# Attention with a decay gate and a Gelu feed-forward on one core: one fused, interleaved pipeline in place of two stages with a DRAM hand-over

## The chip, the cores and the metric

The kernel runs on one core of a Trainium2 chip. The core has TensorE (PE; its weight loads are shown apart, as PEld), VectorE (DVE), ScalarE (ACT), GpSimd (POOL) and SyncE (SP), and 16 DMA engines that the queues of SP and POOL share. The metric is the device time in microseconds; that of the kernel before is 622.77 us, the median of 3 runs (622.64 to 623.76).

## The reference

Attention runs over 8 batches of 8 heads, 576 tokens of 64 numbers each; its output, as 4608 rows of 512, goes through two matrix products with an exact Gelu between them. Inputs and output are float32.

```python
scores = scale * np.matmul(q, k.transpose(0, 1, 3, 2))          # scale = 1/8
cum = np.cumsum(np.log(np.clip(f, 0.0001, 1.0)), axis=-1)
decay = cum[:, :, :, None] - cum[:, :, None, :]
scores = np.where(causal, -1000000000.0, scores + decay)
attn = softmax(scores)                                           # over keys
x = np.matmul(attn, v).transpose(0, 2, 1, 3).reshape(4608, 512)
out = gelu(x @ w_in) @ w_out                                     # 512 -> 2048 -> 512
```

The row term of the decay, `cum` of the query, cancels in the softmax, so a kernel needs only the key's term, exp(-cum).

## The kernel before

It has a short start and two stages. The order of the instructions on each engine is chosen by the framework's scheduler, not by the source.

**Start.** `f` is loaded, ACT takes the logarithm (L68), DVE makes the running sum in ten shifted additions (L72), and five transposes put its negative into `neg_cumT`, keys on partitions (L83, L86).

**Attention**, one head at a time, 64 heads. POOL's queue loads q, k and v with a cast to bf16, one DMA each, in rows of 64 numbers (L122). PE transposes q and k in blocks of 128 tokens (L141), ten transposes a head, and DVE copies them out of PSUM (L146). For each of the five key blocks, four of 128 keys and one of 64, PE computes the scores of the queries from that block on (L158): the contraction is over 64 rows, so the matmuls stand in the profile as 64*128. ACT takes the exponential with `neg_cumT` as a per-partition bias (L166), POOL zeroes the upper triangle of the diagonal block (L173). For each of five query blocks PE sums exp times v, with a 65th column of ones for the row sums, in 15 matmuls of 65 columns a head (L190); DVE divides (L198, L199), and SP stores 64 columns of x in DRAM (L202, L209).

**Feed-forward.** After the last head POOL's queue loads both weight matrices (L223, L224) and SP reads x back through transposing DMAs (L232). Nine chunks of 512 tokens then run one after the other: GEMM1, 16 groups of 4 matmuls of 512 columns (L244), each followed by a Gelu on ACT (L251); GEMM2, 4 groups of 16 such matmuls (L257), each copied out by ACT (L264), and one store of 1 MB a chunk (L265).

Of the kernel before, what the change touches and what calls it, by code (L numbers as in the profile page):

```python
# [10 lines left out]
Exp = mybir.ActivationFunctionType.Exp
Ln = mybir.ActivationFunctionType.Ln
Gelu = mybir.ActivationFunctionType.Gelu
is_ge = mybir.AluOpType.is_ge
# [3 lines left out]
def kernel(  # L19
# [11 lines left out]
    P = 128  # L31

    B, H, S, D = q.shape
# [1 line left out]
    assert D == 64 and S == 576 and BH == 64
# [4 lines left out]
    KB = 128  # L40
    blocks = []
    ss = 0
    while ss < S:
        ns = min(KB, S - ss)
        blocks.append((ss, ns))
        ss += ns
    NB = len(blocks)
# [6 lines left out]
    neg_cumT = consts.tile([P, NB, BH], FP32)

    with tc.tile_pool(name="pre", bufs=1) as pre, tc.tile_pool(
        name="pre_psum", bufs=2, space=bass.MemoryType.PSUM
    ) as pre_psum:
        ident_fp = pre.tile([P, P], FP32)
        make_identity(nc, ident_fp)  # L60
        f_sb = pre.tile([BH, S], FP32)
        nc.sync.dma_start(f_sb, f.rearrange("b h s -> (b h) s"))
        PAD = 512
        c0 = pre.tile([BH, PAD + S], FP32)
        c1 = pre.tile([BH, PAD + S], FP32)
        nc.vector.memset(c0[:, :PAD], 0.0)
        nc.vector.memset(c1[:, :PAD], 0.0)
        nc.scalar.activation(c0[:, PAD:], f_sb, Ln)  # L68
        shift = 1
        src, dst = c0, c1  # L70
        while shift < S:
            nc.vector.tensor_add(  # L72
                dst[:, PAD:], src[:, PAD:], src[:, PAD - shift : PAD - shift + S]
            )
            shift *= 2
            src, dst = dst, src
        cum = src[:, PAD:]
        negcum = pre.tile([BH, S], FP32)
        nc.scalar.mul(negcum, cum, -1.0)
        for n in range(NB):  # L80
            s0, ns = blocks[n]
            ps = pre_psum.tile([P, BH], FP32)
# [216 lines left out]
```

## Time and profile before

| | |
|---|---|
| median of 3 runs | 622.77 us |
| profiled execution, first to last instruction (its span) | 621.1 us |
| what lies around the span, median less span | 1.7 us |
| PE busy | 567.9 us, 91% |
| ACT busy | 272.3 us, 44% |
| POOL busy | 249.7 us, 40% |
| DVE busy | 189.5 us, 31% |
| DMA packets | 191776, of which 184497 under 512 bytes |

The trace holds one execution, and its span is the only time known of that execution itself. Rows of a group by line give line, engine, operation, names and shapes, count, then after the bar the busy time in us, the mean of one in ns, the idle time of the engine just before them and what ended most of it. For a matmul "64*128" is rows times columns of the array in use, and "128x512" the moving operand. The end of a matmul is modelled, so a busy PE is not a PE at its best; the distance from one start to the next says more. In rows of a timeline the first number is the start from the beginning of the span, the second the length, both in us.

### The profile page before, as it was taken

Reading aid. Unit: us, or ns where it says so; the run is one execution under the profiler, and the core shown is the slowest. Engines: PE = TensorE matmul, PEld = TensorE weight load, DVE = VectorE, ACT = ScalarE, POOL = GpSimd, SP = SyncE. Lnnn points to the kernel's source line nnn. Section 1 sums busy time; section 2 is a strip of 40 time slices with the busy share of each in tenths; the row PEclk is TensorE's granted clock in tenths of the full one; section 3 lists DMA queues with packets and bytes.
Section 4 is the critical chain, followed back from the end, with each engine's and each line's share of the span. In section 5 each row is a group of like instructions: output and inputs, shape, how many; then the busy total and the mean of one; then the engine's idle time right before and its main releaser. Section 6 shows DMA issues by size and latency. Waiting matters only on the chain.

```text
span 621.1 us, 9241 instructions
## 1 busy us (share of the span) xinstructions
PE 567.9 (91%) x3118; PEld 289.6 (47%) x3141; DVE 189.5 (31%) x849; ACT 272.3 (44%) x505; POOL 249.7 (40%) x525
## 2 busy tenths in 40 slices
PE   0799999999999999999995069999999999999996
PEld 0355555555555555555552024444444444444442
DVE  6244555556555565555655000000000000000000
ACT  2255455454454554545552043526253443526251
POOL 0989877777777778777742000000000000000000
PEclk9999999999999999999999999999999999999999
DMA  0999999899998889988723985501001010101001
GB/s 10 75 73 76 78 67 69 64 68 67 67 72 64 66 65 69 71 65 66 55 30 61 200 154 97 141 12 68 37 32 69 1 68 1 68 1 68 33 35 69
DMA packets 191776, 39.54 MB, mean 64 GB/s; under 512 B 184497, under 2 KB 186545, under 8 KB 191729
## 3 DMA queue, kind: packets, MB, share of 16 engines
q0 software_dynamic: 128400, 19.91, 43.6%
q1 hardware_dynamic: 63328, 19.04, 13.5%
q8 instruction: 25, 0.41, 0.3%
q14 instruction: 23, 0.18, 0.1%
HBM read 39.94 MB, written 14.16 MB: 87 GB/s over the span
## 4 chain that ended last, share of the span: by engine, by line
PE 89%; DMA 3%; DVE 2%; SPq 2%; ACT 2%; POOL 1%; issue 1%; ACTq 0%; POOLq 0%
PE ps L257 20%; PE ps L244 20%; PE sc L158 18%; PE ps L141 17%; PE o L190 14%; DMA xT_sb<-x_dram 2%; SPq L232 2%; DVE c L72 1%; ACT gT L251 1%; POOL q_bf L122 0%; DMA f_sb<-in_f_dram 0%; POOL k_bf L122 0%; ACT exp_sb L166 0%; POOL v_aug L122 0%; DMA x_dram<-out_head 0%
## 5 line engine op out<-in xcount | busy, mean ns | idle before, releaser
L166 ACT ACTIVATE exp_sb<-sc,neg_cumT 128x576 bf16<-128x576 f32 (+4 forms) x320 | 160.1, 526 | 156.2 <-POOL exp_sb L173 67.2
L244 PE MATMUL ps<-xT_sb,w_in_sb 128*128 128x512 bf16 x565 | 130.5, 383 | 25.8 <-issue 16.2
L158 PE MATMUL sc<-qT,kT 64*128 64x512 bf16 (+5 forms) x384 | 133.5, 410 | 1.2 <-DVE kT L146 0.5
L257 PE MATMUL ps<-w_out_sb,gT 128*128 128x512 bf16 x564 | 125.2, 379 | 0.6
L190 PE MATMUL o<-v_aug,exp_sb 128*128 128x65 bf16 (+2 forms) x960 | 120.9, 244 | 2.3 <-POOL exp_sb L173 1.0
L251 ACT ACTIVATE gT<-ps 128x512 bf16<-128x512 f32 x144 | 85.9, 597 | 42.2 <-PE ps L244 42.2
L244 PEld LDWEIGHTS <-w_in_sb 128*128 128x128 bf16 x576 | 56.1, 97 | 98.6 <-issue 37.5
L190 PEld LDWEIGHTS <-exp_sb 128*128 128x128 bf16 (+2 forms) x960 | 74.9, 131 | 53.6 <-DVE recip L198 26.2
L173 POOL TENSOR_SCALAR_AFFINE_SELECT exp_sb<-exp_sb 128x128 bf16<-128x128 bf16 (+1 forms) x320 | 86.8, 291 | 13.4 <-ACT exp_sb L166 10.0
L199 DVE TENSOR_SCALAR out_head<-o,recip 128x64 bf16<-128x64 f32 (+1 forms) x320 | 88.3, 276 | 5.5 <-DVE recip L198 0.3
L198 DVE RECIPROCAL recip<-o 128x1 f32<-128x1 f32 (+1 forms) x320 | 52.2, 163 | 121.3 <-PE o L190 116.2
L257 PEld LDWEIGHTS <-gT 128*128 128x128 bf16 x576 | 56.3, 98 | 68.0
L122 POOL DMA_DIRECT2D q_bf<-in_q_dram x63 | 54.7, 868 | 61.8 <-PE ps L141 44.4
L141 PE MATMUL ps<-ident_bf,q_bf 128*64 128x128 bf16 (+1 forms) x320 | 65.0, 302 | 3.8 <-issue 3.8
L264 ACT COPY out_sb<-ps 128x512 f32<-128x512 f32 x36 | 21.1, 586 | 102.7 <-PE ps L257 102.7
L141 PE MATMUL ps<-ident_bf,k_bf 128*64 128x128 bf16 (+1 forms) x320 | 58.4, 303 | 0.0
L158 PEld LDWEIGHTS <-kT 64*128 64x128 bf16 (+1 forms) x384 | 38.5, 115 | 39.3 <-issue 17.5
L122 POOL DMA_DIRECT2D v_aug<-in_v_dram x63 | 54.6, 866 | 4.7 <-PE o L190 4.4
L122 POOL DMA_DIRECT2D k_bf<-in_k_dram x63 | 54.5, 866 | 0.4 <-PE sc L158 0.2
L141 PEld LDWEIGHTS <-q_bf 128*64 128x64 bf16 (+1 forms) x320 | 34.2, 142 | 40.2 <-issue 27.5
L141 PEld LDWEIGHTS <-k_bf 128*64 128x64 bf16 (+1 forms) x320 | 33.3, 150 | 11.5 <-issue 3.2
L146 DVE COPY qT<-ps 64x576 bf16<-64x576 bf16 x64 | 28.8, 449 | 10.4 <-PE ps L141 8.7
(29 smaller groups left out, 55.3 us busy)
## 6 DMA issues: line engine op xcount, KB each, us to landing
out_dram<-out_sb SPq DMA_DIRECT2D x9, 1024.0 KB, 4.3
q_bf<-in_q_dram POOLq DMA_DIRECT2D x63, 80.0 KB, 2.9
k_bf<-in_k_dram POOLq DMA_DIRECT2D x63, 80.0 KB, 3.0
v_aug<-in_v_dram POOLq DMA_DIRECT2D x63, 80.0 KB, 2.9
x_dram<-out_head SPq DMA_DIRECT2D x64, 64.0 KB, 2.3
w_in_sb<-in_moe_w_in_dram POOLq DMA_DIRECT2D x1, 2048.0 KB, 13.6
w_out_sb<-in_moe_w_out_dram POOLq DMA_DIRECT2D x1, 2048.0 KB, 25.8
x_dram<-out_head SPq DMA_DIRECT2D x64, 8.0 KB, 1.7
```

What stands on the lines that cost most here:

```text
L122: nc.gpsimd.dma_start(dst, src_ap)
L141: nc.tensor.transpose(ps[:, n * KB : n * KB + ns], bfsrc[:ns, n, :], ident_bf[:ns, :ns],)
L146: nc.vector.tensor_copy(dst[:, :S], ps[:, :S])
L158: nc.tensor.matmul(sc[:ns, q_off : q_off + cw], kT[:D, s0n : s0n + ns], qT[:D, s0n + q_off : s0n + q_off + cw], start=True, stop=True,)
L166: nc.scalar.activation(exp_sb[:ns, :Qc], sc[:ns, :Qc], Exp, bias=neg_cumT[:ns, n : n + 1, bh : bh + 1], scale=scale,)
L173: nc.gpsimd.affine_select(out=exp_sb[:ns, :ns], in_=exp_sb[:ns, :ns], compare_op=is_ge, fill=0.0, base=0, pattern=[[1, ns]], channel_multi ...
L190: nc.tensor.matmul(o[:ms, : D + 1], exp_tiles[n][:ns, col : col + ms], v_aug[:ns, n, :], start=(n == 0), stop=(n == m),)
L198: nc.vector.reciprocal(recip[:ms, :], o[:ms, D : D + 1])
L199: nc.vector.tensor_scalar_mul(out_head[:ms, m, :], o[:ms, :D], recip[:ms, :1])
L244: nc.tensor.matmul(ps, w_in_sb[:, kt, ffb * P : (ffb + 1) * P], xT_sb[:, kt, t0 : t0 + TC], start=(kt == 0), stop=(kt == n_dm - 1),)
L251: nc.scalar.activation(gT[ffb], ps, Gelu)
L257: nc.tensor.matmul(ps2, gT[kt][:, tsub * P : (tsub + 1) * P], w_out_sb[:, kt, :], start=(kt == 0), stop=(kt == n_ff - 1),)
```

## The change

Everything between the constants and the last store is written anew; the lines that go are those printed above. The order on each engine is now that of the source (`manual_schedule`).

- **Loads.** q and k come for a whole batch in one DMA each, 96 partitions by rows of six tokens (384 numbers); v comes as float32 through SP's queue, with its 64 last tokens in a 128-token block from 448 on. Weights are loaded early, in four DMAs each.
- **Decay.** exp(cum at 288 - cum) is made once (a scan on DVE, Exp on ACT, five transposes into `wT`), and POOL multiplies v and the column of ones by it (`weigh_v`), so the exponential of the scores has no bias. All five key blocks have 128 keys; the doubled keys of the last have weight zero.
- **Two heads at a time**, 32 pairs. One transpose takes two tokens of a head, 128 columns on 96 rows (`transposes`), and four strided DVE copies put them in order. k of both heads lies on 128 partitions; q of each head lies on its half, the other half zero (`qA`, `qB`), so that every score matmul contracts over 128 rows. Scores go into four tiles of two PSUM banks, each with one ACTIVATE of up to 1024 numbers (`scores`, `STILES`).
- **x stays on the chip.** `normalize` writes x of a pair, `to_xT` transposes it on PE, and DVE copies it into `xT_sb`. The round trip through DRAM goes.
- **Interleaving.** Batch b's attention is issued with the matmuls of GEMM2 of chunk b-1 between its parts (`take(fill, n)`), then GEMM1 of chunk b with the q and k transposes and the weighing of batch b+1 in it. Chunk 8 follows at the end. GEMM2 is copied out by DVE and stored in 256 KB pieces. ACT so changes between Exp and Gelu twice a batch.

```diff
+STILES = [
+    [(0, 0, 384), (4, 448, 128)],
+    [(1, 128, 448)],
+    [(2, 256, 320), (0, 384, 192)],
+    [(3, 384, 192)],
+]
+SDIAG = [[0, 384], [0], [0], [0]]
...
+    ctx.enter_context(tc.manual_schedule())
...
+    e_pool = ctx.enter_context(tc.tile_pool(name="e", bufs=2))
...
+    s_psum = ctx.enter_context(tc.tile_pool(name="s_psum", bufs=2, space=PSUM))
+    o_psum = ctx.enter_context(tc.tile_pool(name="o_psum", bufs=2, space=PSUM))
+    m_psum = ctx.enter_context(tc.tile_pool(name="m_psum", bufs=2, space=PSUM))
...
+        for src, dst in zip((q, k), qk_of[b]):
+            nc.gpsimd.dma_start(
+                dst[:, h0:h1, :],
+                src[b, h0:h1].rearrange("h (p j) d -> p h (j d)", j=JT),
+            )
...
+        for h in range(h0, h1):
+            nc.sync.dma_start(
+                vt[:, h, 0:4, :],
+                v[b, h, 0:512].rearrange("(n p) d -> p n d", p=P),
+            )
...
+    nc.sync.dma_start(f_sb, f.rearrange("b h s -> (b h) s"))
+    for i in range(HP):
+        load_qk(0, 2 * i, 2 * i + 2)
+    load_v(0)
...
+    for i in range(HP):
+        nc.vector.memset(qA[i][D:P, :], 0.0)
+        nc.vector.memset(qB[i][0:D, :], 0.0)
...
+    for kt in range(n_dm):
+        nc.gpsimd.dma_start(w_in_sb[:, kt, :], w_in_r[:, kt, :])
+    load_qk(1)
+    load_v(1)
+    for kt in range(0, n_ff, 4):
+        nc.gpsimd.dma_start(w_out_sb[:, kt : kt + 4, :], w_out_r[:, kt : kt + 4, :])
...
+    nc.vector.tensor_scalar(f_sb, f_sb, 1e-4, 1.0, Alu.max, Alu.min)
+    nc.scalar.activation(lf, f_sb, Act.Ln)
+    nc.vector.tensor_tensor_scan(cum, ones, lf, 0.0, Alu.mult, Alu.add)
+    nc.scalar.activation(wk, cum, Act.Exp, bias=cum[:, S // 2 : S // 2 + 1], scale=-1.0)
+    psw = o_psum.tile([P, NBLK, BH], FP32, tag="o", name="psw")
...
+    def transposes(b, i, which):
...
+        ps = o_psum.tile([P, 2, JT // 2, PT], BF16, tag="o", name="ps_t")
+        for h in range(2):
+            for j in range(JT // 2):
+                nc.tensor.transpose(
+                    ps[:, h, j, :],
+                    src[:, 2 * i + h, 2 * j * D : 2 * (j + 1) * D],
+                    ident_bf[:PT, :PT],
+                )
+        for h in range(2):
+            dst = (qA[i], qB[i])[h] if which == 0 else kT[i]
+            rows = dst[h * D : (h + 1) * D, :].rearrange(
+                "d (p j two) -> d two p j", j=JT // 2, two=2
+            )
+            for odd in range(2):
+                nc.vector.tensor_copy(
+                    rows[:, odd],
+                    ps[odd * D : (odd + 1) * D, h].rearrange("d j p -> d p j"),
+                )
...
+    def weigh_v(b, i):
...
+        nc.gpsimd.tensor_tensor(
+            vw_of[b][:, hs, :, 0:D],
+            v_of[b][:, hs, :, :],
+            w.unsqueeze(3).to_broadcast([P, 2, NBLK, D]),
+            Alu.mult,
+        )
+        nc.gpsimd.tensor_copy(vw_of[b][:, hs, :, D], w)
...
+    def scores(b, i, t):
+        st = s_psum.tile([P, 2, 512], FP32, tag="s", name=f"s{t}")
...
+        for n, q0, w in STILES[t]:
+            for h, qt in enumerate((qA[i], qB[i])):
+                nc.tensor.matmul(
+                    st[:, h, c : c + w],
+                    kT[i][:, K0[n] : K0[n] + P],
+                    qt[:, q0 : q0 + w],
...
+        nc.scalar.activation(et[:, :, 0:c], st[:, :, 0:c], Act.Exp, scale=scale)
+        for c0 in SDIAG[t]:
+            nc.gpsimd.affine_select(
+                out=et[:, :, c0 : c0 + P],
...
+    def attend(b, i, h, ms):
...
+        for m in ms:
+            for n in range(m + 1):
+                t, c = where(n, m)
+                nc.tensor.matmul(
+                    o[:, m, :],
+                    e_of[b, i, t][:, h, c : c + P],
+                    vw_of[b][:, 2 * i + h, n, :],
...
+    def normalize(b, i, h):
...
+        nc.vector.reciprocal(r, o[:, :, D])
+        nc.vector.tensor_tensor(
+            x_of[b, i][:, :, h, :],
+            o[:, :, 0:D],
+            r.unsqueeze(2).to_broadcast([P, NBLK, D]),
+            Alu.mult,
+        )
+
+    def to_xT(b, i):
+        ps = o_psum.tile([P, S], BF16, tag="o", name="ps_x")
+        for m in (4, 3, 2, 1, 0):
             nc.tensor.transpose(
...
+                ps[:, K0[m] : K0[m] + P], x_of[b, i][:, m, :, :], ident_bf
+            )
+        nc.vector.tensor_copy(xT_sb[:, i, b * S : (b + 1) * S], ps)
...
+        nc.scalar.activation(g_of[c][ffb], ps, Act.Gelu)
...
+    def gemm2(c):
...
+                if kt == n_ff - 1:
+                    ot = o_pool.tile([P, d_model], FP32, tag="ot", name="ot")
+                    nc.vector.tensor_copy(ot, ps)
+                    nc.sync.dma_start(
+                        out[t0 + ts * P : t0 + (ts + 1) * P, :], ot
                     )
...
+                yield
...
+    for i in range(HP):
+        transposes(0, i, 0)
+        transposes(0, i, 1)
+    for n in range(NBLK):
+        nc.tensor.transpose(psw[:, n, :], wk[:, K0[n] : K0[n] + P], ident_fp[:BH, :BH])
+    nc.vector.tensor_copy(wT[:, 0:4, :], psw[:, 0:4, :])
+    nc.vector.tensor_copy(wT[D:P, 4, :], psw[D:P, 4, :])
+    for i in range(HP):
+        weigh_v(0, i)
+
+    for b in range(B):
+        fill = gemm2(b - 1) if b else iter(())
+        load_qk(b + 2)
+        load_v(b + 2)
+        for i in range(HP):
+            for t in range(4):
+                scores(b, i, t)
+                if i:
+                    if t == 0:
+                        attend(b, i - 1, 0, (4, 3))
+                    elif t == 1:
+                        attend(b, i - 1, 0, (2, 1, 0))
+                        normalize(b, i - 1, 0)
+                    elif t == 2:
+                        attend(b, i - 1, 1, (4, 3))
+                    else:
+                        attend(b, i - 1, 1, (2, 1, 0))
+                        normalize(b, i - 1, 1)
+                if i >= 2 and t == 1:
+                    to_xT(b, i - 2)
+                take(fill, 2)
+        i = HP - 1
+        take(fill, 4)
+        attend(b, i, 0, (4, 3, 2, 1, 0))
+        normalize(b, i, 0)
+        to_xT(b, i - 1)
+        take(fill, 4)
+        attend(b, i, 1, (4, 3, 2, 1, 0))
+        normalize(b, i, 1)
+        take(fill, 8)
+        to_xT(b, i)
+        take(fill, 999)
+        for ffb in range(n_ff):
+            gemm1(b, ffb)
+            if b + 1 < B:
+                if ffb % 2 == 1:
+                    transposes(b + 1, ffb // 4, (ffb // 2) % 2)
+                if ffb % 4 == 2:
+                    weigh_v(b + 1, ffb // 4)
+    take(gemm2(B - 1), 999)
+    for c in range(B, n_chunks):
+        for ffb in range(n_ff):
+            gemm1(c, ffb)
+        take(gemm2(c), 999)
```

## Rows read from the trace of the kernel before

**Rows 1.** Page, parts 1, 2, 4: span, engines, granted clock, chain.
```profile
span 621.1 us, 9241 instructions
...
PE 567.9 (91%) x3118; PEld 289.6 (47%) x3141; DVE 189.5 (31%) x849; ACT 272.3 (44%) x505; POOL 249.7 (40%) x525
...
PEclk9999999999999999999999999999999999999999
...
PE 89%; DMA 3%; DVE 2%; SPq 2%; ACT 2%; POOL 1%; issue 1%; ACTq 0%; POOLq 0%
```

**Rows 2.** Windows: stretch, length, busy by engine (count), granted clock, DMA share, GB/s.
```profile
18.50:336.40 317.90, 313.77 (x1984) 176.56 (x1984) 179.96 (x826) 160.08 (x320) 243.73 (x512) 1.00 0.88 65
336.40:364.50 28.10, 3.83 (x7) 1.03 (x9) 0.00 (x0) 1.88 (x3) 1.91 (x2) 1.00 1.11 189
364.50:621.10 256.60, 249.02 (x1122) 111.31 (x1143) 0.00 (x0) 106.42 (x180) 0.00 (x0) 1.00 0.17 52
```

**Rows 3.** Timeline of PE, one head of attention: start, length, line, count.
```profile
154.39 1.03 PE L158 MATMUL sc<-qT,kT 64*128 64x512 bf16 x3
155.35 0.53 PE L141 MATMUL ps<-ident_bf,q_bf 128*64 128x128 bf16 x3
...
158.92 0.40 PE L190 MATMUL o<-v_aug,exp_sb 128*128 128x65 bf16 x4
159.25 0.61 PE L158 MATMUL sc<-qT,kT 64*128 64x512 bf16 x1
```

**Rows 4.** Line L244, 364.5 to 366.2 us, then 367 to 375 us: ns min/median/max.
```profile
L244 PE MATMUL ps<-xT_sb,w_in_sb x4: 586/634/634, 364.6 to 365.8; 128*128 128x512 bf16 x4
...
L244 PE MATMUL ps<-xT_sb,w_in_sb x39: 379/379/379, 366.7 to 374.9; 128*128 128x512 bf16 x39
```

**Rows 5.** Groups by form, PE: busy us, mean ns, idle before, releasers.
```profile
L190 PE MATMUL o<-v_aug,exp_sb 128*128 128x65 bf16 x640 | 81.5, 241 | 2.2 <-POOL exp_sb L173 1.0 <-DVE out_head L199 0.7
...
L257 PEld LDWEIGHTS <-gT 128*128 128x128 bf16 x576 | 56.3, 98 | 68.0
```

**Rows 6.** Chain that ended last, in order: start, length, what.
```profile
348.25 13.67 DMA xT_sb<-x_dram
...
463.01 10.74 PE ps L257 x49
...
615.19 0.59 ACT out_sb L264
```

**Rows 7.** Groups by form, ACT.
```profile
L251 ACT ACTIVATE gT<-ps 128x512 bf16<-128x512 f32 x144 | 85.9, 597 | 42.2 <-PE ps L244 42.2
...
L166 ACT ACTIVATE exp_sb<-sc,neg_cumT 128x576 bf16<-128x576 f32 x64 | 47.4, 741 | 94.2 <-POOL exp_sb L173 64.9 <-PE o L190 17.0 <-PE sc L158 12.3
...
L166 ACT ACTIVATE exp_sb<-sc,neg_cumT 64x64 bf16<-64x64 f32 x64 | 19.8, 310 | 5.1 <-PE sc L158 1.3 <-PE ps L141 0.7 <-PE o L190 0.3
...
L251 ACT ACT_TABLE_LOAD x1 | 1.3, 1283 | 31.3 <-PE ps L244 31.3
```

**Rows 8.** Groups by form, POOL.
```profile
L173 POOL TENSOR_SCALAR_AFFINE_SELECT exp_sb<-exp_sb 128x128 bf16<-128x128 bf16 x256 | 74.4, 304 | 11.7 <-ACT exp_sb L166 9.1
...
L122 POOL DMA_DIRECT2D q_bf<-in_q_dram x63 | 54.7, 868 | 61.8 <-PE ps L141 44.4 <-PE ps L83 13.8 <-PE o L190 3.2
...
L173 POOL TENSOR_SCALAR_AFFINE_SELECT exp_sb<-exp_sb 64x64 bf16<-64x64 bf16 x64 | 15.3, 239 | 1.7 <-ACT exp_sb L166 1.0 <-DVE recip L198 0.3
```

**Rows 9.** Groups by form, DVE.
```profile
L198 DVE RECIPROCAL recip<-o 128x1 f32<-128x1 f32 x256 | 42.0, 164 | 69.0 <-PE o L190 65.0
...
L146 DVE COPY qT<-ps 64x576 bf16<-64x576 bf16 x64 | 28.8, 449 | 10.4 <-PE ps L141 8.7 <-PE sc L158 0.6
...
L86 DVE COPY neg_cumT<-ps 128x64 f32<-128x64 f32 x4 | 0.7, 220 | 1.6 <-PE ps L83 1.6
```

**Rows 10.** DMA issues: count, KB each, median us to landing.
```profile
w_out_sb<-in_moe_w_out_dram POOLq DMA_DIRECT2D x1, 2048.0 KB, 25.8
```

**Rows 11.** Timeline of the start: start, length, engine, line.
```profile
3.71 0.68 ACT L68 ACTIVATE c<-f_sb 64x576 f32<-64x576 f32 x1 [1.63 <-DMA f_sb<-in_f_dram]
```

More of the change, by code (lines that the diff above doesn't have):

```diff
@@ L11, with where @@
 BF16 = mybir.dt.bfloat16
[L12 to L15, printed above, removed]
+Act = mybir.ActivationFunctionType
+Alu = mybir.AluOpType
+PSUM = bass.MemoryType.PSUM
+P = 128
+S = 576
+D = 64
+H = 8
+HP = 4
+NBLK = 5
+K0 = [0, 128, 256, 384, 448]
+TC = 512
+JT = 6
+PT = 96
+STILES = [
[5 more added lines that the diff above has]
+SDIAG = [[0, 384], [0], [0], [0]]
+def where(n, m):
+    q = K0[m]
+    for t, parts in enumerate(STILES):
+        c = 0
+        for nn, q0, w in parts:
+            if nn == n and q0 <= q and q + P <= q0 + w:
+                return t, c + q - q0
+            c += w
+    raise KeyError((n, m))
 @with_exitstack
@@ L30 @@
     nc = tc.nc
[L31 to L33 removed]
+    B = q.shape[0]
+    assert tuple(q.shape) == (B, H, S, D)
     BH = B * H
[L35 removed]
     d_model, d_ff = moe_w_in.shape
     N_tok = B * S
[L40 to L47, printed above, removed]
+    n_dm = d_model // P
+    n_ff = d_ff // P
+    n_sub = TC // P
+    n_chunks = N_tok // TC
     scale = 1.0 / (D ** 0.5)
+    ctx.enter_context(tc.manual_schedule())
@@ L51 @@
+    f_sb = consts.tile([BH, S], FP32)
+    nc.sync.dma_start(f_sb, f.rearrange("b h s -> (b h) s"))
+    for i in range(HP):
+        load_qk(0, 2 * i, 2 * i + 2)
+    load_v(0)
     ident_bf = consts.tile([P, P], BF16)
     make_identity(nc, ident_bf)
[L54 to L73, printed above, removed]
-            )
[L75 to L82, printed above, removed]
@@ new lines, in to_xT, with gemm1 @@
+        nc.vector.tensor_copy(xT_sb[:, i, b * S : (b + 1) * S], ps)
+    g_of = {}
+    def gemm1(c, ffb):
+        t0 = c * TC
+        ps = m_psum.tile([P, TC], FP32, tag="m", name="ps1")
+        for kt in range(n_dm):
+            nc.tensor.matmul(
+                ps,
+                w_in_sb[:, kt, ffb * P : (ffb + 1) * P],
+                xT_sb[:, kt, t0 : t0 + TC],
+                start=(kt == 0),
+                stop=(kt == n_dm - 1),
+            )
+        if c not in g_of:
+            g_of[c] = [
+                g_pool.tile([P, TC], BF16, tag=f"g{n}", name=f"g{n}")
+                for n in range(n_ff)
+            ]
+        nc.scalar.activation(g_of[c][ffb], ps, Act.Gelu)
@@ new lines, in take @@
+    def take(gen, n):
+        for _ in range(n):
+            if next(gen, "end") == "end":
+                return
+    for i in range(HP):
[46 more added lines that the diff above has]
+                    weigh_v(b + 1, ffb // 4)
```

255 lines of the change are left out of this document (82 added, 173 removed).

## The prediction

> **What bounds the kernel now.** I read the page first. PE is busy for 91% of 621.1 us and the chain that ended last is 89% PE; no other engine passes 44% [rows 1]. The windows by stage come next: attention takes 317.9 us with PE busy throughout, then 28.1 us in which PE stands almost still while DMA runs at 189 GB/s, then 256.6 us of feed-forward [rows 2]. In the standstill the chain shows the transposing read of x, 13.67 us in one piece [rows 6].
>
> A busy PE says little, so I read the distance from start to start. In GEMM2 49 matmuls take 10.74 us [rows 6]; without the last one's modelled 0.38 that is 10.36 / 48 = 0.216 us for 512 columns, 2.37 columns a ns, the 2.4 GHz level. In attention three score matmuls of 512, 64 and 448 columns start at 154.39 and the next instruction at 155.35 [rows 3]: 1024 columns in 0.96 us, 1.07 a ns, the 1.2 GHz level. The granted clock reads full in both [rows 1, 2]. Line L244 decides which to believe: its first four matmuls of the stage last 586 to 634 ns, 39 of the same shape right after last 379 [rows 4]. Before the rise PE ran those back to back; before them it had waited for DMA. So the clock row cannot be right before about 366 us, and I take attention to run wholly at 1.2 GHz: one head every 4.86 us [rows 3].
>
> The feed-forward has nothing to give: 1152 matmuls x 0.216 = 248.8 of its 256.6 us. The change can win the standstill and up to half of attention.
>
> **The change part by part.** I sum PE at 2.4 GHz over a middle batch, then add the waits of its in-order queue.
>
> GEMM1 and GEMM2: 128 x 0.216 = 27.65 us. Scores: the tiles hold 512, 448, 512 and 192 columns for each of two heads, 3328 a pair, 4 pairs: 13312 / 2.37 = 5.6 us. Exp times v: still 15 matmuls of 65 columns a head, 120 a batch. Four take 0.40 us at the low level, so a step is (0.40 - 0.24) / 3 = 0.053 us, the last one's 0.24 being the mean length [rows 3, 5]. At the high level it is at least 65 / 2.4 = 0.027, and 0.053 if something other than the columns sets it; I take 0.040: 4.8 us (3.2 to 6.4). Weight loads last 98 ns [rows 5] but the step of 53 shows them overlapping; if at the high clock they did not, that is a rival. Transposes of x: 20 x 128 columns, 1.1 us. Transposes of q and k: 48 x 96 columns, 1.9 us, with 16 changes between 128 and 96 rows. A change of shape costs 0.96 - 1024 / 1.2 = 0.107 us at the low level [rows 3]; between nothing and that I take 0.08: 1.3 us. Sum 42.4 us a batch.
>
> The Trainium skill (TensorE: Matmul & The Clock Gate, section Back-to-back issue gap) gives about 81 ns for a matmul of 128 columns in a stream of weight loads and matmuls. By that the 960 small matmuls would add 960 x 0.041 = 39 us and the sum would be 484. This trace disagrees: 53 ns, at the lower clock.
>
> Waits on ACT. Its cost per column is (741 - 310) / 512 = 0.842 ns, and an ACTIVATE without a per-partition bias is cheaper, 597 at 512 columns against 687 on that line [rows 7]. Without the bias 1024, 896, 1024 and 384 numbers cost 1.03 + 0.92 + 1.03 + 0.49 = 3.47 us a pair (3.83 with it), 14 a batch; with 16 x 0.60 of Gelu, 24, below PE. But each batch changes tables twice, 1.28 us each, and the load waits for PE's result (31.3 us of idle before it end at PE's L244) [rows 7], so both lie where PE soon needs ACT. After GEMM1 the last Gelu ends at about 0.8, the table at 2.1, pair 0's exponentials at 5.5, POOL's last triangle at 6.0; PE by then has only pair 0's scores, the first of pair 1's and 8 fill matmuls, (3328 + 1024) / 2.37 + 8 x 0.216 = 3.6 us. Queued behind PE's first waiting matmul is everything else it has: 2.4 us lost. At the first Gelu, 0.86 + 1.28 + 0.60 + 0.2 = 2.9 against PE's need of that bank at 2.2: 0.8 lost. For the last triangle of each pair, which lands about when PE wants it, I allow 0.3 a pair, 1.2. Together 4.4 us a batch (1.5 if ACT runs closer behind, 9 if every pair waits 1.5).
>
> The Trainium skill (ScalarE: Activation LUTs, section Rules for kernel authors) budgets about 2.7 us for each change of table set and says to batch by set. By that 15 changes would add 15 x 1.4 = 21 us, 466 in all; the trace has 1.283 us for the load itself.
>
> DVE. The four copies after each transpose group move 288 numbers in 4-byte steps, a form the trace does not have. Contiguous bf16 goes at (449 - 164) / 575 = 0.50 ns a number, float32 at (220 - 164) / 63 = 0.89 [rows 9]; 0.31 to 0.42 us a copy, 0.68 at twice the slower pace. I take 0.42 as nearest for strided numbers: 4 x 0.42 + 0.2 = 1.9 us, hidden behind two GEMM1 groups and the next transposes, 8 x 0.216 + 0.4 = 2.1 us. The cover is thin; without it, below.
>
> POOL. A triangle of 256 numbers costs 304 + 128 x 1.02 = 434 ns [rows 8], 20 a batch: 8.7 us. `weigh_v` multiplies 640 numbers by a second operand: 0.83 us at that pace, 2.4 at three times it; I take 1.5, four a batch. With the loads, 2 x 0.87 or a little more [rows 8] where there were 24, POOL needs some 17 of 47 us: nothing on the path, and behind its loads stand only triangles that come later. If a triangle came 0.4 us late for every pair, that would be 13 us; the 0.3 a pair above holds part of it. SP's v loads stand ahead of the stores and wait for buffers freed a batch ago. DMA has the same bytes of input in rows of 1536 bytes instead of 256, v excepted, and no x: its share of 0.88 in attention [rows 2] goes, at no gain of its own, since PE set that pace; nor is there a new cost while it stays under 1.
>
> So batches 1 to 7 take 7 x (42.4 + 4.4) - 3.2 (no transposes in the last) = 324.4 us.
>
> Start and batch 0. `f` is on the chip at 3.71 and ACT's Ln takes 0.68 [rows 11], but DVE first fills nine constants, estimated at 576 x 0.89 = 0.5 us each [rows 9]; scan done at about 9. Then 32 strided copies, 13.4 us, stand on DVE ahead of everything: 22.5. Weights' transposes and copies: 24. Four `weigh_v` on POOL ahead of the first triangles: 30; five triangles: 32. Without fill PE may stay at 1.2 GHz: (3328 + 30 x 65 + 5 x 128) / 1.2 = 4.9 us a pair, three pairs: 47; last sums, division and transposes: 50.5. GEMM1 of chunk 0: 13.8 + 3.2 + 0.8, and 1.7 for eight matmuls before the rise as in [rows 4]: 70. The bounds are 52 (copies at 0.31, weighing at 0.83, full clock) and 85 (the decay's PSUM slot, held from before the transposes, leaves them one buffer and each group waits for the last: 8 x 2.6). Loads ahead of GEMM1, 11 MB of float32, are hidden if they keep the pace of the two weight loads before, 8 MB by 25.8 us after the second was issued [rows 10]: 36 us against 50. At half that pace PE would wait 20 us once.
>
> End. GEMM2 of chunk 7 and chunk 8: 192 x 0.216 = 41.5, two waits for a last Gelu 2; the copy and store after PE took 5.9 us from 615.19 to the end [rows 6], with a smaller store 5.5. Together 49.
>
> The span: 70 + 324.4 + 49 = 443.4. Median and span differ by 1.7 us before, which I keep: **445 us**. Its own range, from the bounds above, is 415 to 480.
>
> **The rivals.**
> Weight loads set the pace. If the 98 ns of a load [rows 5] cannot overlap 27 ns of columns, 960 x (0.098 - 0.040) adds 56: 501. For it: each such matmul has its own load. Against: steps of 53.
> DVE sets the pace of GEMM1. At 0.68 a copy a group takes 2.9 us against 2.1: 56 x 0.8 = 45, and 8 at the start: 498. For it: the thin cover. Against: it needs twice the slowest pace seen.
> The clock stays down, the other side. The 42.4 us of each batch double, 297 more, and the 31 us of waits vanish in it: 711. It is slower than before once 178 of those 297 us of PE work run at 1.2 GHz. For it: attention now does, though PE hardly pauses. Against: 512-column matmuls on 128 rows had it up within seven or so and held it [rows 4, 6], and they stand between all parts of the new attention. A half form, with only the 25.4 us of attention and GEMM2 of each batch at 1.2 GHz, adds 178 less 25 of waits: 598.
> Shorter than 415: small matmuls at 0.027 (-12), waits of 1.5 (-20), start 52 (-18).
>
> **How the numbers follow.** Forecast 0.66, weight loads 0.10, DVE 0.08, clock down everywhere 0.06, in half 0.04, under 415 0.06. The range 408 to 510 takes in the first three and some of the last. Within 0.2%, about what a measurement of this kernel can tell from no change, lies only a sliver of the half form, 0.01; slower 0.06; faster 0.93.
>
> **What would show it.** PE's 65-column step at 30 to 45 ns, not 98. 512-column lengths of 379 in every batch from 1 on, also between parts of attention; 600 there would mean the clock rival. Two table loads a batch, with PE idle 1 to 3 us before the second pair's first sums. DVE's strided copies near 0.42 us. GEMM1 of chunk 0 ending near 70 us and batches 47 us apart. Batches of 53 or more with the clock up mean one of the first two rivals.

## The result and the profile after

The changed kernel takes 419.34 us, the median of 5 runs (418.57 to 421.05), against 622.77 (622.64 to 623.76, 5 runs): a ratio of 0.6736, 95% interval 0.6722 to 0.675. The forecast was 445 us, so faster than forecast by 6%, and inside the forecast's own range. The traced execution is the longest of the five (421.05 us, span 419.1; the spans of the others are 416.6 to 418.0).

Page of the changed kernel: span, engines, granted clock, chain.

```profile
span 419.1 us, 7515 instructions
...
PE 368.4 (88%) x3045; PEld 207.5 (50%) x3045; DVE 207.2 (49%) x466; ACT 215.0 (51%) x291; POOL 129.5 (31%) x262
...
PEclk9999969999999999999999999999999999999999
...
PE 77%; ACT 8%; POOL 5%; issue 4%; DVE 4%; ACTq 0%; POOLq 0%
```

Against [rows 1], PE's busy time falls by 199.5 us with 2% fewer matmuls, and its share only from 91 to 88%. The chain still runs on PE for 77%; ACT and POOL, 3% together before, now hold 13% of it: PE waits for them. The clock row has one dip near 60 us and otherwise reads full; by [rows 4] that row has to be checked against durations, and the groups below do so.

Windows by stage (stretch, length, busy by engine with counts, granted clock, DMA share, GB/s): attention of batch 0, GEMM1 of chunk 0, then for a middle batch GEMM1 and attention with GEMM2, and the end.

```profile
0.00:57.80 57.80, 22.27 (x241) 15.89 (x242) 27.17 (x65) 18.46 (x21) 28.82 (x57) 0.98 1.13 189
57.80:75.60 17.80, 17.80 (x109) 8.85 (x107) 13.38 (x29) 8.96 (x15) 5.44 (x9) 0.87 0.56 126
188.40:204.10 15.70, 15.70 (x108) 8.04 (x106) 13.67 (x29) 8.96 (x15) 0.81 (x1) 1.00 0.43 101
204.10:231.10 27.00, 25.45 (x259) 15.65 (x258) 11.20 (x28) 16.37 (x19) 14.15 (x29) 1.00 0.39 75
373.50:419.10 45.60, 41.66 (x193) 18.65 (x191) 5.53 (x8) 10.15 (x17) 0.00 (x0) 0.98 0.13 47
```

These answer [rows 2]. The standstill of 28.1 us is gone, and 317.9 us of attention and 256.6 of feed-forward have become 57.8 + 17.8, seven batches of 42.6 on average (75.6 to 373.5 us), and 45.6. In the middle batch PE is idle for only 1.55 of its 42.7 us. What is left is the start: there PE is busy for 22.27 of 57.8 us.

Groups by form (line, engine, operation, names, shapes, count, then busy us, mean ns, idle before and its releasers).

```profile
L297 PE MATMUL ps<-w_out_sb,g 128*128 128x512 bf16 x576 | 146.2, 379 | 0.0
...
L222 POOL TENSOR_SCALAR_AFFINE_SELECT e<-e 128x256 bf16<-128x256 bf16 x160 | 62.5, 406 | 114.7 <-ACT e L220 114.3
...
L181 DVE COPY kT<-ps_t 64x288 bf16<-64x288 bf16 x128 | 61.3, 479 | 2.5 <-PE ps_t L170 0.3
...
L241 PE MATMUL o<-vw,e 128*128 128x65 bf16 x960 | 53.9, 196 | 17.7 <-POOL e L222 9.7 <-POOL vw L201 7.0 <-DVE x L255 0.5
...
L241 PEld LDWEIGHTS <-e 128*128 128x128 bf16 x960 | 45.5, 99 | 29.7 <-POOL e L222 11.3 <-issue 7.6 <-DVE x L255 2.5
...
L289 ACT ACT_TABLE_LOAD x8 | 10.3, 1283 | 0.1
```

The first row holds all 576 matmuls of GEMM2 at a mean of 379 ns, the length that [rows 4] has after the clock's rise: the clock is up between the parts of attention too.

Timeline of PE in a middle batch (start, length, line, count), in attention and then in GEMM1.

```profile
212.12 0.45 PE L241 MATMUL o<-vw,e 128*128 128x65 bf16 x9
212.41 0.59 PE L297 MATMUL ps<-w_out_sb,g 128*128 128x512 bf16 x2
212.84 0.25 PE L210 MATMUL s<-qA,kT 128*128 128x192 bf16 x1
```

```profile
190.19 0.42 PE L170 MATMUL ps_t<-ident_bf,q 96*128 96x96 bf16 x6
190.45 1.89 PE L277 MATMUL ps<-xT_sb,w_in_sb 128*128 128x512 bf16 x8
192.18 0.42 PE L170 MATMUL ps_t<-ident_bf,k 96*128 96x96 bf16 x6
```

The rows give the steps. Nine sums of 65 columns: (0.45 - 0.196) / 8 = 0.032 us. Two GEMM2 matmuls: 0.43 / 2 = 0.215. Six 96-column transposes: 0.26 us to the next line, 0.043 each, and the eight 512-column matmuls behind them 1.73 / 8 = 0.216: a change between 96 and 128 rows adds nothing that can be seen.

### The profile page after: what moved, and what is told of

Its sections match the earlier page's. It is cut to its first block, busy times and chain, and to the rows that moved or that the text cites. A ratio compares the mean times of both kernels' runs of the same rounds, so it can differ in the third digit from the quotient of the medians.

```text
span 419.1 us, 7515 instructions
## 1 busy us (share of the span) xinstructions
PE 368.4 (88%) x3045; PEld 207.5 (50%) x3045; DVE 207.2 (49%) x466; ACT 215.0 (51%) x291; POOL 129.5 (31%) x262
## 4 chain that ended last, share of the span: by engine, by line
PE 77%; ACT 8%; POOL 5%; issue 4%; DVE 4%; ACTq 0%; POOLq 0%
PE ps L277 30%; PE ps L297 26%; PE s L210 7%; PE o L241 7%; ACT e L220 6%; PE ps_t L170 4%; POOL e L222 3%; PE ps_x L265 2%; DVE kT L181 2%; ACT L220 1%; DVE qB L181 1%; DVE qA L181 1%; POOL vw L195 1%; POOL q L98 1%; POOL k L98 1%
## 5 line engine op out<-in xcount | busy, mean ns | idle before, releaser
L289 ACT ACTIVATE g<-ps 128x512 bf16<-128x512 f32 x144 | 86.0, 597 | 125.7 <-PE ps L277 125.7
L297 PE MATMUL ps<-w_out_sb,g 128*128 128x512 bf16 x576 | 146.2, 379 | 0.0
L220 ACT ACTIVATE e<-s 128x1024 bf16<-128x1024 f32 (+2 forms) x128 | 105.7, 862 | 56.2 <-PE s L210 47.6
L222 POOL TENSOR_SCALAR_AFFINE_SELECT e<-e 128x256 bf16<-128x256 bf16 x160 | 62.5, 406 | 114.7 <-ACT e L220 114.3
L241 PE MATMUL o<-vw,e 128*128 128x65 bf16 x960 | 53.9, 196 | 17.7 <-POOL e L222 9.7
L297 PEld LDWEIGHTS <-g 128*128 128x128 bf16 x576 | 49.4, 98 | 37.8
L210 PE MATMUL s<-qA,kT 128*128 128x384 bf16 (+2 forms) x192 | 54.6, 289 | 11.3 <-ACT e L220 10.3
L181 DVE COPY kT<-ps_t 64x288 bf16<-64x288 bf16 x128 | 61.3, 479 | 2.5 <-PE ps_t L170 0.3
L241 PEld LDWEIGHTS <-e 128*128 128x128 bf16 x960 | 45.5, 99 | 29.7 <-POOL e L222 11.3
L210 PE MATMUL s<-qB,kT 128*128 128x384 bf16 (+2 forms) x192 | 49.7, 290 | 0.0
## 6 DMA issues: line engine op xcount, KB each, us to landing
w_out_sb<-in_moe_w_out_dram POOLq DMA_DIRECT2D x4, 512.0 KB, 25.7
```

What stands on the lines that cost most here:

```text
L181: nc.vector.tensor_copy(rows[:, odd], ps[odd * D : (odd + 1) * D, h].rearrange("d j p -> d p j"),)
L210: nc.tensor.matmul(st[:, h, c : c + w], kT[i][:, K0[n] : K0[n] + P], qt[:, q0 : q0 + w], start=True, stop=True,)
L220: nc.scalar.activation(et[:, :, 0:c], st[:, :, 0:c], Act.Exp, scale=scale)
L222: nc.gpsimd.affine_select(out=et[:, :, c0 : c0 + P], in_=et[:, :, c0 : c0 + P], compare_op=Alu.is_ge, fill=0.0, base=0, pattern=[[0, 2], [ ...
L241: nc.tensor.matmul(o[:, m, :], e_of[b, i, t][:, h, c : c + P], vw_of[b][:, 2 * i + h, n, :], start=(n == 0), stop=(n == m),)
L289: nc.scalar.activation(g_of[c][ffb], ps, Act.Gelu)
```

## The experiments

Two questions were open. What holds the clock up: the scores on 128 rows (theory 1), or GEMM2's matmuls between the parts of attention (theory 2)? And what takes 57.8 us at the start: the weights' traffic ahead of v (theory A), or DVE's 32 copies (theory B)? The runs down to `a_half_nofill` go with the first question; `a_fill6` asks what the wait behind a table load is worth; `a_actcopy`, `a_loads` and `a_loads_act` go with the second question, and the last two put the gains together.

**a_rows64.** Each head's scores on its own 64 rows, as in the kernel before.

```diff
-                    kT[i][:, K0[n] : K0[n] + P],
-                    qt[:, q0 : q0 + w],
+                    kT[i][h * D : (h + 1) * D, K0[n] : K0[n] + P],
+                    qt[h * D : (h + 1) * D, q0 : q0 + w],
```

> The changed kernel, but each head's score matmuls contract over its own 64 rows again instead of 128 rows half of which meet zeros. Theory 1 (the clock follows how the attention's own matmuls fill the rows): TensorE drops to 1.2 GHz in attention, the 25 us of attention and GEMM2 in each batch double in whole or in part, 470 to 570 us. Theory 2 (the 512-column GEMM matmuls between the parts keep the clock up, whatever the scores do): clock stays up; two heads on disjoint halves of the rows may overlap, up to 2.8 us a batch less, 397 to 419 us; if each change between 64 and 128 rows costs 0.1 us as in the kernel before, 430 to 455 us.

Measured: 418.96 us, 0.6723 (0.671 to 0.6735): no difference. Timeline of PE, same columns:

```profile
211.46 0.59 PE L297 MATMUL ps<-w_out_sb,g 128*128 128x512 bf16 x2
211.99 0.33 PE L210 MATMUL s<-qA,kT 64*128 64x384 bf16 x1
211.99 0.33 PE L210 MATMUL s<-qB,kT 64*128 64x384 bf16 x1
...
212.31 0.50 PE L241 MATMUL o<-vw,e 128*128 128x65 bf16 x9
```

The clock stayed up without 128-row scores. The rows explain the equal time. Scores of the two heads now start together, so a batch's 5.6 us of score columns shrink to 2.8. But the second GEMM2 matmul starts at 211.46 + 0.216 = 211.68 and the scores at 211.99: 0.31 us where 0.216 is due, 95 ns for the change from 128 to 64 rows. The way back costs about the same: 512 columns of each head, side by side, are due 0.21 us, and the sums start 0.32 us later. A batch has 16 score tiles and so 32 such changes, 3.0 us. The zero rows of `qA` and `qB` cost as much as they save.

**b_rows128.** The kernel before with its scores on 128 rows, rows 64 to 127 of q and k zero, and nothing else.

```diff
+    Tz = [consts.tile([P, S], BF16, name=f"Tz{i}") for i in range(6)]
+    for tz in Tz:
+        nc.vector.memset(tz[D:P, :], 0.0)
...
-            qT = T_pool.tile([D, S], BF16, tag="T")
-            kT = T_pool.tile([D, S], BF16, tag="T")
+            qT, kT = Tz[2 * bh % 6], Tz[(2 * bh + 1) % 6]
...
-                nc.vector.tensor_copy(dst[:, :S], ps[:, :S])
+                nc.vector.tensor_copy(dst[:D, :S], ps[:, :S])
...
-                        kT[:D, s0n : s0n + ns],
-                        qT[:D, s0n + q_off : s0n + q_off + cw],
+                        kT[:, s0n : s0n + ns],
+                        qT[:, s0n + q_off : s0n + q_off + cw],
```

> The kernel before with one part of the change alone: q and k transposed lie in tiles of 128 rows whose upper half is zero, so the score matmuls contract over 128 rows; columns and order stay. Theory 1: TensorE leaves 1.2 GHz in attention, a head falls from 4.86 us to what POOL needs, 3 x 0.868 + 4 x 0.304 + 0.239 = 4.06 us, 64 x 0.8 = 51 us less, about 572 us. Theory 2 (it takes the GEMM matmuls in between): clock stays down, no change beyond a few us, 615 to 627 us.

Measured: median 602.57 us; three runs at 602.40 to 602.88, against 622.83 a ratio of 0.967 to 0.968, and one at 593.5, so that the ratio with its interval came out as 0.96 (0.9516 to 0.9684). That one run has a mean granted clock of 0.773 in its record where the others have 0.998 or 0.999; it has no trace, and why it differs stays open. Timeline of PE, one head and the small scores before it, then the same small scores in the kernel before:

```profile
156.34 0.45 PE L160 MATMUL sc<-Tz,Tz 128*128 128x320 bf16 x1
...
156.86 0.37 PE L192 MATMUL o<-v_aug,exp_sb 128*128 128x65 bf16 x3
...
157.83 1.04 PE L160 MATMUL sc<-Tz,Tz 128*128 128x512 bf16 x3
158.80 0.53 PE L143 MATMUL ps<-ident_bf,q_bf 128*64 128x128 bf16 x3
...
162.51 1.04 PE L160 MATMUL sc<-Tz,Tz 128*128 128x512 bf16 x3
```

```profile
157.58 0.45 PE L158 MATMUL sc<-qT,kT 64*128 64x320 bf16 x1
...
158.45 0.34 PE L190 MATMUL o<-v_aug,exp_sb 128*128 128x65 bf16 x3
```

A head takes 162.51 - 157.83 = 4.68 us, 0.18 less than in [rows 3], and 1024 columns still take 0.97 us, 1.06 a ns: the low level. The last two pairs of rows each hold 320 columns of scores, two sums of 65 and 192 columns of scores. With three changes of rows they take 0.87 us, without any 0.52: about 0.12 us a change at the low level. PE gives part of that back in waits for ACT (13.3 us in all ahead of its score matmuls), and 64 x 0.18 = 11.5 us remain. About 6 of the other 9 lie in the standstill before the feed-forward, where PE waits 18.6 us in one piece, for the load of `w_in`, and in the kernel before 24.3 us in four; that was not followed further. In the traced execution theory 1 by itself falls: 128-row scores do not raise the clock in the old order. Whether they did for a part of the run at 593.5 us cannot be told.

**a_nofill.** All of GEMM2 ahead of the batch's attention instead of between its parts.

```diff
         load_v(b + 2)
+        take(fill, 999)
         for i in range(HP):
```

> The changed kernel with all of GEMM2 of the chunk before issued ahead of a batch's attention, none of it between its parts. Theory 1: attention keeps the clock up by itself and each batch is paced by ACT, 4 x 3.4 + 1.3 and some tails, about 18.5 us plus 13.8 of GEMM2 instead of 27.0: 5 us a batch more, about 454 us. Theory 2: the clock drops in each attention, a pair takes 4.9 us or more, and GEMM1 begins low: 490 to 510 us.

Measured: 475.78 us, 0.7623 (0.7596 to 0.7649). Windows of one batch, GEMM2 and then attention:

```profile
223.40:237.40 14.00, 13.89 (x69) 6.52 (x70) 4.47 (x8) 0.60 (x1) 0.77 (x1) 1.00 0.75 142
237.40:258.40 21.00, 14.48 (x190) 10.22 (x190) 7.27 (x20) 15.67 (x18) 11.22 (x25) 0.92 0.04 13
```

Attention alone takes 21.0 us, in which ACT is busy for 15.67 and PE for 14.48: neither fills it, they wait for each other, and the clock dips (0.92). The time lies between what the two theories gave (454, and 490 to 510), 22 us above theory 1's: the size of PE's waits without cover was missed. The dip is short, and attention ends it by itself: matmul lengths rise at 242.4 us, after waits for ACT, and fall back by 245.5, with no GEMM2 between. Interleaving is worth 475.78 - 419.34 = 56 us, waits and dips together.

**a_half.** Both heads' scores on the first 64 rows, so that the second head's are those of the first; GEMM2 stays between.

```diff
-                    kT[i][:, K0[n] : K0[n] + P],
-                    qt[:, q0 : q0 + w],
+                    kT[i][0:D, K0[n] : K0[n] + P],
+                    qA[i][0:D, q0 : q0 + w],
```

> The changed kernel with the score matmuls of both heads on array rows 0 to 63, so that they can neither overlap nor fill 128 rows; the second head's scores are those of the first (left out). Theory 1 (half-filled rows bring the clock down): rows of 512 columns in attention last 600 ns, 470 to 570 us. Theory 2 (the clock holds, half-filled rows only cost their columns again and the changes of shape): against the run with each head on its own rows 2.8 us a batch of lost overlap, 8 batches, 22 us: about 441 us.

Measured: 439.8 us, 0.7061 (0.7048 to 0.7075). Window of attention and GEMM2 in one batch:

```profile
214.70:243.80 29.10, 28.18 (x260) 13.64 (x259) 11.17 (x28) 16.70 (x19) 14.27 (x29) 1.00 0.36 69
```

The clock is full with half the rows in use and no overlap of the heads: GEMM2 between the parts suffices. The 2.1 us above the changed kernel's 27.0 are no more than the changes of shape, 32 x 0.095 = 3.0, would give. Batch 0 of the same trace, which has no GEMM2 to put between, is the opposite case: there 1024 columns of scores take 0.96 us (50.37 to 51.33 us), the low level, though the clock row reads full, and GEMM1 starts at 63.39 us instead of 57.84. With full rows, in the changed kernel, lengths fall to the high level in that stretch, at 45.2 us.

**a_half_nofill.** Both edits: half rows (the second head's scores again those of the first) and no GEMM2 between.

```diff
+        take(fill, 999)
...
+                    kT[i][0:D, K0[n] : K0[n] + P],
+                    qA[i][0:D, q0 : q0 + w],
```

> Both edits at once: the score matmuls of both heads on array rows 0 to 63 (the second head's scores are those of the first), and all of GEMM2 ahead of a batch's attention. Theory X (128-row scores or GEMM2 in between, either is enough to keep the clock, neither leaves it as in the kernel before): the clock falls in the whole of each attention, a pair takes (3328 + 30 x 65 + 5 x 128) / 1.2 = 4.9 us and its changes of shape, 5.5 instead of 3.5 to 4: about 475 + 8 x 7 = 530 us. Theory Y (the denser order keeps it by itself): as without GEMM2 in between, plus at most the 2.8 us a batch of the half rows where PE and not ACT paces: 475 to 497 us.

Measured: 533.9 us, 0.8562 (0.8549 to 0.8574). Windows of one batch's attention and of the next batch's GEMM2:

```profile
214.90:242.00 27.10, 24.00 (x188) 13.87 (x189) 7.04 (x20) 14.84 (x18) 13.46 (x28) 0.50 0.01 3
256.40:270.00 13.60, 13.49 (x68) 6.29 (x68) 4.32 (x8) 0.60 (x1) 0.77 (x1) 1.00 0.79 146
```

Now the low level is there, 0.50 through all of attention, and attention takes 27.1 us where `a_nofill` took 21.0. Each of the two alone, full rows or GEMM2 between, kept the clock at 0.92 or above; without both it falls. So theories 1 and 2 are both half right for the new order, and in the old order full rows were not enough. What else kept it down there, perhaps its 64-column transposes or its changes of shape, was not tried.

**a_fill6.** Six GEMM2 matmuls, not two, after each of the first two score tiles of a batch.

```diff
-                take(fill, 2)
+                take(fill, 6 if i == 0 and t < 2 else 2)
```

> The changed kernel with 6 instead of 2 GEMM2 matmuls after each of the first two score tiles of a batch, 8 taken from the batch's end. If PE's 2.5 us of waits at a batch's start are ACT's table load and first exponentials, with nothing else behind, 8 x 0.216 = 1.7 us a batch go, 7 batches: about 407 us. Rival: ACT stays behind by the same amount and the wait comes back at the next pair's sums: 415 to 419 us.

Measured: 409.86 us, 0.6586 (0.657 to 0.6602). Window of attention and GEMM2 in one batch:

```profile
197.00:222.70 25.70, 25.12 (x255) 15.67 (x259) 11.35 (x29) 16.43 (x19) 14.15 (x29) 1.00 0.41 78
```

25.7 us against 27.0, with PE's busy time nearly the same: the wait behind the table load is covered. 7 x 1.3 = 9 us, the measured difference of 9.5. Here the same matmuls in another place are worth 2%.

**a_actcopy.** Half of batch 0's strided copies on ACT, which is idle there (theory B's test).

```diff
-                nc.vector.tensor_copy(
-                    rows[:, odd],
-                    ps[odd * D : (odd + 1) * D, h].rearrange("d j p -> d p j"),
-                )
+                part = ps[odd * D : (odd + 1) * D, h].rearrange("d j p -> d p j")
+                if b == 0 and odd:
+                    nc.scalar.copy(rows[:, odd], part)
+                else:
+                    nc.vector.tensor_copy(rows[:, odd], part)
```

> The changed kernel with half of batch 0's copies out of PSUM (one of two a head) on ACT instead of DVE. Theory A (the start waits for v's last load, which lands at 33.3 us because small packets of v share the DMA engines with 4 MB of weights): DVE is done 7 us earlier and nothing follows from it, 417 to 420 us. Theory B (the start is paced by DVE's 32 copies, as the prediction had it): 7 us less, about 412 us.

Measured: 419.1 us, 0.6733 (0.6708 to 0.6757): no gain. Rows of DVE and POOL at the start:

```profile
20.52 0.23 DVE L325 COPY wT<-psw 64x64 f32<-64x64 f32 x1
...
33.34 1.28 POOL L196 TENSOR_TENSOR vw<-v,wT 128x640 bf16<-128x640 f32 x1 [13.22 <-issue]
```

DVE's last copy into `wT` ends at 20.75 us instead of 24.44, and the weighing still starts at 33.34. Theory B falls as the first limit.

**a_loads.** The same loads in another order: `w_in` is held until q and k of three pairs are transposed, q, k and v of batch 1 come inside batch 0's attention, `w_out` after them, batch 2 last.

```diff
-    for kt in range(n_dm):
-        nc.gpsimd.dma_start(w_in_sb[:, kt, :], w_in_r[:, kt, :])
-    load_qk(1)
-    load_v(1)
...
+        if i == 2:
+            gate = consts.tile([P, 1], BF16, name="gate")
+            nc.gpsimd.tensor_copy(gate, kT[2][:, 0:1])
+            for kt in range(n_dm):
+                nc.gpsimd.dma_start(w_in_sb[:, kt, :], w_in_r[:, kt, :])
...
-        load_qk(b + 2)
-        load_v(b + 2)
+        if b:
+            load_qk(b + 2)
+            load_v(b + 2)
...
+            if b == 0 and i == 1:
+                load_qk(1)
+                load_v(1)
+            if b == 0 and i >= 2:
+                for kt in (8 * i - 16, 8 * i - 12):
+                    nc.gpsimd.dma_start(
+                        w_out_sb[:, kt : kt + 4, :], w_out_r[:, kt : kt + 4, :]
+                    )
...
+        if b == 0:
+            load_qk(2)
+            load_v(2)
```

> The changed kernel with the loads in another order: w_in is issued only once the third pair's keys are transposed (about 18 us), q, k, v of batch 1 and w_out inside batch 0's attention, those of batch 2 at its end. Theory A: v of batch 0 lands before 24 us, the weighing starts with the decay at 24.4 instead of 33.4, and 8 to 10 us go: about 410 us. Theory B: DVE sets the start, nothing goes: 417 to 420 us. If w_in or w_out now come late for GEMM1 or GEMM2 of chunk 0, up to 10 us come back.

Measured: 409.36 us, 0.657 (0.6558 to 0.6581). Timeline of POOL at the start:

```profile
24.56 1.28 POOL L189 TENSOR_TENSOR vw<-v,wT 128x640 bf16<-128x640 f32 x1 [2.76 <-DVE wT L323]
...
30.07 1.84 POOL L216 TENSOR_SCALAR_AFFINE_SELECT e<-e 128x256 bf16<-128x256 bf16 x5
```

The weighing starts at 24.56 us instead of 33.39 and is released by DVE's `wT`, no longer by the load; the first triangle runs at 30.07 instead of 40.48. 10.4 us, and the time falls by 10.0. Of the 10.4 us 8.8 are the earlier start of the weighing; the other 1.6 are the two loads of batch 2, which POOL no longer issues between the weighing and the triangle. Theory A holds, and DVE's copies are now what comes next. All later loads were moved at once, so which of them held v back is not told apart.

**a_loads_act.** The edits of `a_actcopy` and `a_loads`, unchanged, in one kernel.

> Both of the two edits before together: with v early, DVE's copies become what the weighing waits for, so halving them now counts: 5 to 7 us less than the run with the loads alone, about 404 us. If the sum is no less than with the loads alone, something third sets the start.

Measured: 405.52 us, 0.6509 (0.6487 to 0.6532); the weighing starts at 20.84. With the loads out of the way, ACT's help that was worth nothing by itself gives 3.8 us.

**a_best.** `a_loads_act` and `a_fill6` together.

> The three edits that won, together: loads in the new order, half of batch 0's copies on ACT, 6 instead of 2 GEMM2 matmuls after the first two score tiles of a batch. They act on different stretches, so 405.5 - 9.5 = 396 us; if two of them had taken the same wait away, 399 to 405.

Measured: 394.65 us, 0.6331 (0.6319 to 0.6343). The gains add: 405.52 - 9.5 = 396.0.

**a_best64.** `a_loads_act`, each head's scores on its own 64 rows, and two score tiles at a time, so that a batch has 16 changes of shape, not 32.

```diff
-            for t in range(4):
-                scores(b, i, t)
+            for h in range(2):
+                scores(b, i, 2 * h)
+                scores(b, i, 2 * h + 1)
                 if i:
...
+                    attend(b, i - 1, h, (4, 3, 2, 1, 0))
+                    normalize(b, i - 1, h)
...
-                take(fill, 2)
+                take(fill, 12 if i == h == 0 else 6 if i else 4)
...
-        take(fill, 8)
+        take(fill, 4)
```

> Loads and ACT copies as in the run before, and each head's scores on its own 64 rows with two tiles issued at a time, so that the overlap of the two heads (2.8 us a batch) is had for half the changes of shape (16 instead of 32 a batch, 0.095 us each, 1.5 us); GEMM2 is dealt out as 12, 4, then 6 matmuls. If the changes of shape are all it costs, 1.3 us x 8 less than the run before: about 386 us. Rival: two tiles at a time make PE wait for ACT's PSUM buffers, 0.3 to 0.5 us a pair: 394 us or more.

Measured: 383.16 us, 0.6145 (0.6135 to 0.6155), 0.914 of the changed kernel. Windows of one batch, GEMM1 and then attention with GEMM2:

```profile
161.50:177.40 15.90, 15.70 (x108) 8.05 (x108) 13.84 (x30) 8.96 (x15) 2.32 (x4) 1.00 0.42 100
177.40:201.50 24.10, 23.82 (x256) 12.73 (x259) 11.17 (x28) 16.11 (x19) 12.69 (x27) 1.00 0.44 83
```

A batch takes 40.0 us with PE idle for 0.48 of them, and 24.1 of attention against 27.0. The overlap saves 2.8 us a batch and the 16 changes cost 16 x 0.095 = 1.5, so these two are worth some 1.3 of the 2.9 us. The placement of GEMM2 was changed with them, and how much each gave was not measured apart.

## Why the prediction was right, and where its sizes were off

The mechanism held at each step that the trace can show: attention's clock doubled, the round trip of x went, PE sets the pace. By parts the sum was 70 + 324.4 + 49 = 443.4 us and the trace has 75.6 + 297.9 + 45.6 = 419.1: +5.6, -26.5 and -3.4.

One bound of the prediction was passed: "the standstill and up to half of attention" is 28.1 + 159 = 187 us, and the span fell by 202. Half of attention leaves out the changes of shape. A head's 3727 columns before (1600 of scores, 975 of sums, 1152 of transposes) take 3.1 us at 1.2 a ns; about a dozen changes at 0.12 us would make up most of the rest of its 4.86. That is an estimate from the rows of `b_rows128`. Nearly all of these changes are gone in the new order.

**The batches: 46.8 forecast, 42.6 measured.** Three terms were mis-sized, all taken inside their bounds where the trace came out nearer the better end. The 65-column step is 0.032 us, not 0.040: 120 x 0.008 = 1.0 us. A change between 96 and 128 rows costs nothing, not 0.08: 1.3 us. The steps of PE then sum to about 40.0. That leaves 42.6 - 40.0 = 2.6 us of waits, not 4.4 (PE's busy time, whose ends are modelled, shows less idle than the steps do). The rule of the Trainium skill (TensorE: Matmul & The Clock Gate, section Back-to-back issue gap) of about 81 ns for a matmul of 128 columns in a stream does not hold in this trace: five transposes of x, of 128 columns each and each with its own weight load, take 0.27 us (227.39 to 227.66 us), 54 ns each, and the sums of 65 columns 32. The price of a change, 0.107 us, came near what a change of rows between 64 and 128 costs (0.12 us in the kernel before, 95 ns at full clock in `a_rows64`), but by luck: at the place in [rows 3] that it was read from, `b_rows128` has 0.97 us for the same 1024 columns with no change of rows, only one from 128 to 64 columns of the array. A batch of the new order has neither kind of change.

**The tables.** Forecast: both loads lie where PE soon needs ACT, 2.4 and 0.8 us lost. Timeline of ACT and PE where Gelu gives way to Exp:

```profile
204.30 0.60 ACT L289 ACTIVATE g<-ps 128x512 bf16<-128x512 f32 x1 [0.27 <-PE ps L277]
...
205.06 1.28 ACT L220 ACT_TABLE_LOAD   x1 [0.17 <-PE s L210]
...
206.36 3.17 ACT L220 ACTIVATE e<-s 128x1024 bf16<-128x1024 f32 x4
207.43 0.30 PE L210 MATMUL s<-qA,kT 128*128 128x320 bf16 x1 [1.23 <-ACT e L220]
```

The last Gelu ends at 204.90, the load runs to 206.34, the first exponential follows, and PE waits 1.23 us for it; with the later tiles about 2.0, near the 2.4. The size is near by luck, for the wait is at another place: the prediction let PE run on to the second pair's first sums, but the third score tile of the first pair already needs one of the two PSUM buffers back, and so the first exponential. The other load costs nothing. The forecast let it wait for PE's result, as [rows 7] shows it; the group of L289 above has 0.1 us of idle time ahead of eight loads: here it runs as soon as the last exponential is done, beside PE's remaining GEMM2, and is over 8.0 us before the first Gelu has its data. The Trainium skill (ScalarE: Activation LUTs, section Rules for kernel authors) budgets about 2.7 us for a change of set. The load itself is 1.283 us in this trace as in the one before, and `a_fill6` got back 1.3 of the 2.0 us that it cost.

**The start: 70 forecast, 75.6 measured.** "Loads ahead of GEMM1, 11 MB of float32, are hidden if they keep the pace of the two weight loads before" is the step that failed: GEMM1 did not wait, but the weighing, put at 24 us, did. Timeline of POOL at the start, then of PE:

```profile
33.39 1.28 POOL L195 TENSOR_TENSOR vw<-v,wT 128x640 bf16<-128x640 f32 x1 [13.08 <-issue]
...
38.88 0.83 POOL L98 DMA_DIRECT2D q<-in_q_dram  x1
...
40.48 0.77 POOL L222 TENSOR_SCALAR_AFFINE_SELECT e<-e 128x256 bf16<-128x256 bf16 x2
```

```profile
34.89 0.32 PE L241 MATMUL o<-vw,e 128*128 128x65 bf16 x3 [7.01 <-POOL vw L201]
42.37 0.51 PE L241 MATMUL o<-vw,e 128*128 128x65 bf16 x6 [7.16 <-POOL e L222]
...
57.84 3.62 PE L277 MATMUL ps<-xT_sb,w_in_sb 128*128 128x512 bf16 x8
61.25 0.69 PE L170 MATMUL ps_t<-ident_bf,q 96*128 96x96 bf16 x6
```

The first weighing starts at 33.39. Four of them with their columns of ones, 1.27 + 0.22 less overlap each, and two more loads on POOL's own queue stand ahead of the first triangle at 40.48, and PE waits 7.01 and 7.16 us. The load behind it, from the DMA view of its issue (count, KB, us to landing), and the windows of the start and of the dip:

```profile
v<-in_v_dram SPq DMA_DIRECT2D x1, 256.0 KB, 25.0
```

```profile
8.00:33.00 25.00, 9.01 (x62) 5.62 (x60) 15.84 (x34) 4.26 (x5) 6.42 (x10) 1.00 1.19 200
55.50:62.30 6.80, 5.98 (x36) 3.35 (x37) 1.78 (x5) 1.19 (x2) 5.45 (x8) 0.50 0.82 183
```

The last piece of v for batch 0, issued at 8.30 us, took 25.0 us to land, with the DMA engines full (share 1.19, 200 GB/s) of weights and of batch 1's q and k, none of which was needed before 57 us. DVE was done with `wT` at 24.44, near the 24 forecast. The prediction had weighed the loads by bytes against GEMM1's start only, and not by which of them shares the engines with v; and it saw no new cost for DMA while its share stays under 1, which it does not at the start. `a_loads` shows the cause and its price, 10 us, of which 8.8 are v. Part of it was given back: the three pairs, put at 4.9 us each at the low clock, took about 3.7 (45.92 to 49.60 us), since matmul lengths fall at 45.2 us, inside attention of batch 0. The 1.7 us for a low clock at GEMM1's start did come: from 55.5 to 62.3 us the clock is low, and the first eight matmuls take 3.41 us (57.84 to 61.25) where 1.73 are due at full clock. In `a_actcopy`, whose mean clock reads 1.0, the same eight take 1.79, so it does not come in every execution.

**The end: 49 forecast, 45.6 measured.** The row of PE's last work in the chain:

```profile
401.35 13.83 PE ps L297 x64
```

64 matmuls take 13.83 us, 0.216 each. From PE's end at 415.18 the copy and store take 3.9 us, not 5.5, and most of the rest of the difference is the two waits for a last Gelu, forecast at 2: 192 x 0.216 = 41.5 of the 41.7 us before the copy are matmuls.

**DVE and POOL.** The strided copy takes 0.479 us, above the 0.42 taken and far below the 0.68 at which it would have set the pace: four and the idle between come to 1.96 us, and PE shows no wait for them in GEMM1. The cover was as thin as the prediction feared: PE's own step, two GEMM1 groups and six transposes, is 1.99 us (190.19 to 192.18). `weigh_v` takes 1.28 us (1.5 taken), a triangle 0.406 (0.434). POOL is busy for 14.15 + 0.81 us of a batch's 42.7.

**The rivals.** Weight loads still last 99 ns and do not set the pace of a 32 ns step. DVE does not bound GEMM1. The clock is up. With neither full rows nor GEMM2 between, it would have been low in attention: `a_half_nofill` comes nearest to the half form of that rival. Its 533.9 us lie below the 598 worked out for the half form, since only attention ran at the low level, with GEMM2 ahead of it at full clock.
